# An adaLN block with cached attention and a gated FFN: Q's weight sums and splits at other steps, two kinds of work on another engine, background jobs over other steps, and four stores for the last weight rows

## The chip, the cores and the metric

The kernel runs on one core of a Trainium2 chip. The metric is the device time of one execution in microseconds (us), as the median of several executions. A core has a tensor engine for matmuls (PE in the profile; PEld is its loading of stationary operands), a vector engine (VectorE, DVE), a scalar engine (ScalarE, ACT), GpSimd (POOL) and SyncE (SP), which here issues nearly all DMA transfers. Each engine works through its own instructions in program order and waits on semaphores for the others. SBUF is the on-chip memory of 128 partitions, PSUM the matmuls' accumulator, and DRAM tiles serve as scratch. Transfers are carried out by 16 DMA engines.

## The reference

The input x is 2048 x 576, the attention has 32 query heads on 16 key heads of 128 columns with only the last 512 cached keys, and the FFN has 4608 hidden columns. All is float32.

```
W = min(4096, max(256, Sk // 4))                       # 512
q = (x @ wq).reshape(B, Sq, Hq, Dh), heads first
scores = einsum("bhqd,bhkd->bhqk", q, k[last W]) * Dh ** -0.5
o = einsum("bhqk,bhkd->bhqd", softmax(scores), v[last W]);   A = o @ wo
B(h) = (sigmoid(h @ w_gate) * (h @ w_up)) @ w_down

sa, ca, ga, sb, cb, gb = (silu(c) @ w_mod) in six rows of 576
h = layernorm(x) * (1 + ca) + sa
x = x + ga * A(h)
h = layernorm(x) * (1 + cb) + sb
x = x + gb * B(h)
```

## The kernel before

**Precision.** A float32 product is made of three matmuls in a faster type: each operand is split into a rounded high part (hi, a copy on ScalarE) and what is left (lo, a subtraction on GpSimd or VectorE), and `three` (line 283) multiplies hi by lo, lo by hi and hi by hi. So every matrix that goes to TensorE costs a copy and a subtraction somewhere.

**The step loop.** Attention works in 128 blocks (a head and a quarter of the rows, 512 of them); a block has four steps of 128 rows, so the loop (line 1297) runs over steps n from -8 to 512 and a few behind. In a step come, in program order: the functions that `at_n` hung on this step; Q matmuls (`u_some`); `scores(n + 2)` with the row maximum (neg) on VectorE; `transp(n)`, which transposes the probabilities and splits them into hi and lo (ptt); `expo(n + 2)`, the exponential (pp) on ScalarE, with the row sums; `pv` in two of four steps, probabilities times V into the tile ot, and after its second half VectorE's product of ot with rb, the broadcast of 1/sum, into ov; then the functions that `at_late` hung on the step. `keep_order` and `pin` tell the scheduler to keep an instruction in program order, so an engine's queue is in the main the order of this code, and all that follows an instruction that waits, waits too.

**1/sum.** At the end of a block VectorE takes the reciprocal (rs). `put_rs` stores it to DRAM (rscr, `at_late(n - 2)`, that is the end of the step in which it is made) and `get_rs` reads it back to all partitions (rb, two steps later). SyncE issues both, and rb waits for rscr to land.

**Q.** From the third block pair on, Q is made in units (30, one every 16 steps, `b_of` gives the first block) of seven products, after Strassen and Winograd, in place of eight. A unit u has a start step n = 4 b_of(u) - 10. `u_load` and `u_load_tail` fetch its columns of wq (tiles q and tr), `u_sum` makes the four weight sums S1 to S4 on GpSimd, `u_sum_tail` that of the last rows (tr), `u_tail_hi` and `u_tail_lo` split them (tw), `u_hi` and `u_lo` split the operands of product j into a tile sw of a ring of four. Line 864 and on hangs these on steps around n. `u_some` issues the products' matmuls by the table QUOTA, into the PSUM tiles qp and wo. When product j is done, `u_end` moves m1, u2, w aside or adds two of them into c; `u_out` copies c into Q's hi part (qt) and subtracts for the lo part, on VectorE for j = 4 and on GpSimd for 5 and 6.

**Background jobs.** The weights of the later phases are prepared in the shadow of attention, in three tiles of the size of x (rooms; tile x in the profile). A job "ab" (36 of them) loads a 128-column chunk of w_gate and w_up, makes four sums of it on GpSimd and stores seven planes (tile wsc in DRAM); a job "tail" (9) does so with the last 32 rows of each half for four chunks at once, with the hi and lo split done ahead; "wo" (16) and "down" (18), called wide, multiply by a modulation row, make sums, split, and store to wosc and dsc; "mod" (4) makes a modulation row: a load of w_mod, then ScalarE multiplies by silu(c) and GpSimd adds the products (`mod_sum`). `bg_load`, `bg_sums`, `bg_split` and `bg_store` are hung on steps after the job's start. A planner (line 1106 and on) gives each job a start step and a room: LIFE is the number of steps for which a room is held (and the step from which a wide job needs a second room), held_rooms what is taken otherwise, and `due` spaces the jobs.

**A tail job's stores** (line 1088). The four chunks lie side by side on 32 partitions each. Chunk q's rows go to four places in its tile of DRAM scratch, hi and lo in turn; lo needs two transfers (3 and 4 planes), so a part is six transfers, and the four parts stand in four steps, n + 9 to n + 12:

```
for to in range(4):
    for a, b, src in bg_pairs(k) if to % 2 else [(0, 7, hi)]:
        pin(nc.sync.dma_start(wsc[f + q][to * TQ : (to + 1) * TQ, a:b, 2, :], src[rows]))
```

**The end of the loop.** x is loaded again into the rooms; at N - 7 (N = 512) the pool wp is closed and a pool for the next phase opens, whose first operands `v_load`, `v_sum` and `v_split` prepare. For the last heads `sum_o` makes three sums on GpSimd. Behind the loop come the output projection (to 1950 us of the span) and the FFN, which the change leaves as they are.

The helper class at line 24 issues the instructions, so the profile puts nearly all of them down to L36; the tiles' names tell them apart.

Of the kernel before, what the change touches and what calls it, by code (L numbers as in the profile page):

```python
# [16 lines left out]
P = 128  # L17
# [27 lines left out]
def adaln_block_kernel(ctx: ExitStack, tc: tile.TileContext, x, k_cache, v_cache, wq, wo, w_gate, w_up, w_down,  # L45
# [100 lines left out]
    def mod_load(m, room):  # L146
        ws = []
        for j in range(2):
            w = bg_view(room, j * NC * D2, [NC, D2])
            cols = slice(m * D + j * D2, m * D + (j + 1) * D2)  # L150
            keep_order(nc.sync.dma_start(w, w_mod[: NC * P, cols].rearrange("(k p) n -> p k n", p=P)))
            ws.append(w)
        t = h_tile("wmt")[:TAIL]
        keep_order(nc.sync.dma_start(t, w_mod[NC * P :, m * D : (m + 1) * D]))
        return ws, t

    def mod_sum(loaded, k):
        ws, t = loaded
        for j in range(2):
            w = ws[j][:, k, :] if k < NC else t[:, j * D2 : (j + 1) * D2]  # L160
            kk = w.shape[0]
            keep_order(nc.scalar.activation(w, w, AF.Copy, scale=cexp[:kk, k : k + 1]))
            if k:
                nc.gpsimd.tensor_add(ws[j][:kk, 0, :], ws[j][:kk, 0, :], w)

    def mod_half(row, j, add, loaded):
        p = ps_pt()[:, :D2]
        pin(nc.tensor.matmul(p, ones, loaded[0][j][:, 0, :], start=True, stop=True))
        nc.vector.tensor_scalar(row[:, j * D2 : (j + 1) * D2], p, add, None, op0=OP.add)
# [503 lines left out]
    def expo(n):  # L673
# [5 lines left out]
        if i == TPB - 1:  # L679
            RS[b] = at.tile([P, TPB], F32, tag="rs", name="rs", bufs=3)  # L680
            nc.vector.reciprocal(RS[b], SUM[b])
            if b < NBLK - 2:
                at_late(n - 2, put_rs, b)
                at_late(n, get_rs, b)
# [3 lines left out]
            if last_of[half * H + hd] == b:  # L688
                if not summed(half, hd):
                    at_late(n + (2 if b == NBLK - 1 else 4), put_o, half, hd)  # L690
                elif hd % 2 == 0:
                    at_n(n + 4, sum_o, hd + 1)
                    at_n(n + 7, put_sx, hd + 1, (0, 1))
# [74 lines left out]
    def sum_o(hd):  # L768
# [4 lines left out]
        pin(nc.gpsimd.tensor_sub(s2, s1, e[:, :, 0]))  # L773
        pin(nc.gpsimd.tensor_sub(e[:, :, 1], e[:, :, 0], e[:, :, 1]))
# [136 lines left out]
    for b in range(2, NB):  # L911
        at_n(n1 - 60 + 4 * b, x_room, b)
        at_n(n1 + 40, x_room_end, b)
        for t in range(TPB):
            at_n(n1 - 59 + 4 * b + t, load_x, b, t)
# [92 lines left out]
    wsc = [dram.tile([P, 7, 3, P], F32, tag=f"wsc{f}", name=f"wsc{f}") for f in range(NF)]  # L1008
# [10 lines left out]
    def bg_load(k, rooms):  # L1019
        kind, f = k  # L1020
        if kind == "tail":
            raw = bg_view(rooms[0], 0, [4, P])
            BG[k] = raw, bg_view(rooms[0], 4 * P, [4, P]), bg_view(rooms[0], 8 * P, [7, P])
            for slot, w, r0 in ((0, w_gate, 2 * P), (1, w_gate, D2 + 2 * P), (3, w_up, 2 * P), (2, w_up, D2 + 2 * P)):
# [16 lines left out]
    def bg_sums(k, part):  # L1041
        kind, f = k
        if kind in ("ab", "tail"):
            if kind == "tail":
                r, m, hi = BG[k]
                x0, x1, x2, x3 = [r[:, i] for i in range(4)]
                s1, s2, s4, s3 = [m[:, i] for i in range(4)]
            else:
                x0, x1, x2, s1, s2, s4, s3, x3 = [BG[k][:, i] for i in range(8)]
# [19 lines left out]
        pin(nc.gpsimd.tensor_sub(t1, b12, b11))  # L1069
        pin(nc.gpsimd.tensor_sub(t2, b22, t1))  # L1070
        pin(nc.gpsimd.tensor_sub(t3, b22, b12))
        pin(nc.gpsimd.tensor_sub(t4, b21, t2))

    def bg_pairs(k):
        r, m, hi = BG[k]
        return [(0, 3, r[:, 0:3, :]), (3, 7, m)]

    def bg_split(k, part):
        if k[0] == "tail":
            r, m, hi = BG[k]  # L1080
            a, b, v = ((0, 3, r[:, 0:3]), (3, 7, m))[part]
        else:
            a, b = ((0, 4), (4, 8 if k == ("down", NF // 2 - 1) else 7))[part]
            v, hi = BG[k][0][:, a:b], BG[k][1]
        pin(nc.scalar.activation(hi[:, a:b].bitcast(F32R), v, AF.Copy))
        pin(nc.gpsimd.tensor_sub(v.bitcast(F32R), v, hi[:, a:b]))
# [19 lines left out]
    LIFE = {"ab": (9, None), "tail": (13, None), "wo": (11, 6), "down": (11, 6), "mod": (12, None)}  # L1106
    held_rooms = {0: [(-99, 29), (n1 - 53, n1 + 1)], 1: [(-99, 22), (n1 - 49, n1 - 6)],
                  2: [(-99, 25), (n1 - 26, n1)]}
    plan = []

    def room_for(a, b, but=None):
        fits = [(max([e for s, e in held_rooms[r] if e <= a], default=0), r) for r in held_rooms
                if r != but and all(e <= a or s >= b for s, e in held_rooms[r])]
        return max(fits)[1] if fits else None

    mods = [("gate1", 2, 0.0), ("scale", 4, 1.0), ("shift", 3, 0.0), ("gate", 5, 0.0)]
    mod_at, mod_due = {}, [30, 52, 80, 116]
    n, due = 22, 22.0
    while jobs or wide or mods:
# [743 lines left out]
```

## Time and profile before

| what | value |
| --- | --- |
| time, median of 3 runs | 3202.26 us (3201.67 to 3204.27) |
| the profiled execution's own time | 3205.68 us |
| its span in the profile | 3203.9 us |
| granted TensorE clock, mean | 0.986 |
| DMA over the span | 571.40 MB, 178 GB/s |
| HBM read / written | 394.33 MB / 173.70 MB |

The span is divided into the step loop (to about 1610 us), the output projection (to 1950 us) and the FFN. Busy time says how much of the span an engine executed something; the idle time in front of an instruction is put down to the one that released it last ("<-"). The granted clock is the share of full speed at which TensorE was allowed to run. DMA shares are of the core's 16 DMA engines.

### The profile page before, as it was taken

How to read it: one execution, taken by the hardware profiler on the slowest of the kernel's cores; microseconds unless marked ns; L12 is line 12 of the kernel's file. 1: busy time of each engine (PE TensorE's matmuls, PEld its weight loads, DVE VectorE, ACT ScalarE, POOL GpSimd, SP SyncE). 2: the span in 40 equal slices, each digit the busy share in tenths (PEclk: the TensorE clock that was granted, in tenths of full speed). 3: DMA queues.
4: the chain of work that ended last, by engine and by line, in shares of the span. 5: the costliest groups of instructions: out<-in, count | busy, mean ns of one | idle time of the engine just before them, and what ended most of it. 6: DMA issues, size and time to landing. Idle time of an engine off the chain costs nothing.

```text
span 3203.9 us, 50611 instructions
## 1 busy us (share of the span) xinstructions
PE 3052.6 (95%) x16981; PEld 2610.6 (81%) x16981; DVE 2190.0 (68%) x3845; ACT 1749.0 (55%) x3658; POOL 1914.0 (60%) x1836
## 2 busy tenths in 40 slices
PE   9988999899999898989999999999999999999999
PEld 7776777777777776767799998888888888888888
DVE  7666666687776665657678877666666686666667
ACT  5666566567666555555544465444444554444443
POOL 5566676634767767776255513676665566656565
PEclk9999999999999999999999999999999999999999
DMA  4575766662676766667754765655555565555554
GB/s 113 161 206 173 216 191 197 197 181 62 197 210 197 205 191 199 203 200 227 226 184 176 306 234 170 192 159 167 167 144 147 157 196 146 147 144 142 144 139 121
DMA packets 465636, 571.40 MB, mean 178 GB/s; under 512 B 51040, under 2 KB 414048, under 8 KB 456672
## 3 DMA queue, kind: packets, MB, share of 16 engines
q1 hardware_dynamic: 464240, 567.64, 59.5%
q8 instruction: 134, 2.20, 0.3%
q14 instruction: 126, 1.03, 0.1%
q10 hardware_dynamic: 1136, 0.53, 0.1%
HBM read 394.33 MB, written 173.70 MB: 177 GB/s over the span
## 4 chain that ended last, share of the span: by engine, by line
PE 49%; DVE 1%; POOL 1%; issue 0%; DMA 0%; ACT 0%; SPq 0%; DVEq 0%; POOLq 0%; ACTq 0%
PE a L36 20%; PE w L36 13%; PE c L36 10%; PE b L36 5%; PE ot L36 0%; DVE x L36 0%; PE st L36 0%; POOL x L36 0%; DVE v L36 0%; DMA rb<-rscr 0%; DVE sw L36 0%; POOL vs L36 0%; POOL hl L36 0%; DVE ov L36 0%; DVE ptt L36 0%
## 5 line engine op out<-in xcount | busy, mean ns | idle before, releaser
L36 DVE TENSOR_TENSOR x<-w,x 128x288 f32<-128x288 f32 x964 | 420.7, 451 | 249.2 <-PE w L36 248.1
L36 PE MATMUL a<-hc,sw 128*128 128x512 f32 x2016 | 583.5, 395 | 1.6 <-DVE v L36 1.5
L36 PE MATMUL st<-kt,qt 128*128 128x512 f32 x1536 | 477.6, 414 | 52.8 <-ACT pp L36 50.0
L36 DVE TENSOR_TENSOR ptt<-st,ptt 128x512 fp32r<-128x512 f32 x512 | 351.3, 686 | 213.0 <-ACT ptt L36 211.2
L36 ACT ACTIVATE ptt<-st 128x512 fp32r<-128x512 f32 x512 | 305.1, 596 | 340.0 <-PE st L36 338.0
L36 DVE TENSOR_REDUCE neg<-st 128x1 f32<-128x512 f32 x512 | 350.2, 684 | 151.9 <-PE st L36 149.8
L36 PE MATMUL ot<-ptt,vs 128*128 128x512 f32 (+1 forms) x2052 | 433.0, 352 | 13.7 <-DVE ptt L36 13.3
L36 ACT ACTIVATE pp<-st,neg 128x512 f32<-128x512 f32 x512 | 351.8, 687 | 79.5 <-DVE neg L36 77.9
L36 PEld LDWEIGHTS a<-hc,sw 128*128 128x128 f32 x2016 | 355.9, 188 | 42.3 <-DVE v L36 3.3
L36 PEld LDWEIGHTS st<-kt,qt 128*128 128x128 f32 x1536 | 283.9, 194 | 126.6 <-ACT pp L36 71.5
L36 POOL TENSOR_TENSOR sw<-sr,sw 128x256 fp32r<-128x256 f32 x245 | 198.9, 812 | 283.6 <-ACT sw L36 283.4
L36 PEld LDWEIGHTS ot<-ptt,vs 128*128 128x128 f32 x2052 | 317.1, 192 | 61.4 <-DVE ptt L36 26.2
L36 ACT ACTIVATE sw<-sr 128x384 fp32r<-128x384 f32 x504 | 257.8, 519 | 192.0 <-issue 89.8
L36 POOL TENSOR_TENSOR x<-x 128x288 f32<-128x288 f32 (+5 forms) x369 | 287.7, 795 | 69.2 <-DMA x<-in_B_w_up_dram 41.0
L36 PEld LDWEIGHTS st<-ident,pp 128*128 128x128 f32 x2048 | 260.8, 142 | 79.7 <-issue 4.8
L36 PE MATMUL st<-ident,pp 128*128 128x128 f32 x2048 | 317.4, 276 | 3.2 <-DVE rs L36 2.1
L36 PE MATMUL c<-hc,sw 128*128 128x512 f32 x1008 | 302.7, 393 | 0.0
L36 DVE TENSOR_TENSOR sw<-sr,sw 128x256 fp32r<-128x256 f32 x259 | 189.2, 731 | 142.6 <-ACT sw L36 117.9
L36 POOL TENSOR_TENSOR hl<-vs,hl 128x512 fp32r<-128x512 f32 x139 | 191.5, 1378 | 107.3 <-ACT hl L36 107.3
L36 POOL TENSOR_TENSOR x<-x,x 128x864 fp32r<-128x864 f32 (+3 forms) x111 | 207.4, 1874 | 68.6 <-ACT x L36 39.7
L36 PEld LDWEIGHTS c<-hc,sw 128*128 128x128 f32 x1008 | 181.5, 188 | 18.7
L36 PE MATMUL wo<-hTm,sw 128*128 128x512 f32 x540 | 164.2, 425 | 30.4 <-ACT m L36 15.5
(291 smaller groups left out, 6061.7 us busy)
## 6 DMA issues: line engine op xcount, KB each, us to landing
sr<-wsc SPq DMA_DIRECT2D x504, 192.0 KB
dsc<-x SPq DMA_DIRECT2D x34, 1008.0 KB
vr<-oscr SPq DMA_DIRECT2D x32, 1024.0 KB
rb<-rscr SPq DMA_DIRECT2D x126, 256.0 KB
oscr<-ov SPq DMA_DIRECT2D x63, 512.0 KB
wsc<-x SPq DMA_DIRECT2D x36, 896.0 KB
wosc<-x SPq DMA_DIRECT2D x32, 1008.0 KB
wh<-dsc SPq DMA_DIRECT2D x72, 288.0 KB
```

The lines of the kernel that those rows point to most:

```text
L36: i = got(*args, **kw)
```

## The change

It has these parts.

1. Q's units: loads, sums, tail sums and the splits of the operands stand on other steps. The tail's sum leaves the step of its copy, and the copies for products 0 to 6 go from steps (-4, -3, -1, 0, 3, 6, 8) to (-7, -6, -3, -2, 3, 5, 7) around the unit's start; a low part still comes one step behind.
2. The low part of Q is always made on VectorE (`u_out_lo`); it was on GpSimd for two of three.
3. A modulation row's sum is made by VectorE alone, 5 instructions a row on 576 columns, with one load in place of two, and on later steps.
4. `get_rs` is issued one step earlier.
5. Wide jobs: sums in three steps, splits at +7 and +8, store at +9; tail jobs: splits at +7 and +8, all stores at +9. LIFE and the planner follow: 12 steps for wide, 10 for ab, 11 for tail and mod, and the planner takes the first of a series of spacings with which all jobs end before step N - 30.
6. A tail job's 24 stores become 4, each of which writes one of the four places for all four chunks; the DRAM tiles of four chunks are one tile for that.
7. At the loop's end: x in pieces of a quarter block, the next phase's first load and sums three steps earlier, and `sum_o` over three steps.

```diff
     def mod_sum(loaded, k):
...
+        w, t = loaded
+        if k == 0:
+            pin(nc.vector.tensor_scalar(w[:, 0], w[:, 0], cexp[:, 0:1], None, op0=OP.mult))
+            return
+        v = w[:, k] if k < NC else t
+        a, n = w[: v.shape[0], 0], v.shape[0]
+        pin(nc.vector.scalar_tensor_tensor(a, v, cexp[:n, k : k + 1], a, op0=OP.mult, op1=OP.add))
...
-    def u_out(b, eng):
+    def u_out(b):
         t, c = q_tile(b), u_temp("c")
         keep_order(nc.scalar.activation(t[:, 0, :], c, AF.Copy))
+
+    def u_out_lo(b, c, eng):
+        t = QT[b]
         pin(eng.tensor_sub(t[:, 1, :], c, f32(t[:, 0, :])))
...
-            at_late(n + 3 if j == 6 else n, u_out, b + j - 3, nc.vector if j == 4 else nc.gpsimd)
+            eng = nc.vector
+            m = n + 3 if j == 6 else n
+            at_late(m, u_out, b + j - 3)
+            at_late(m, u_out_lo, b + j - 3, u_temp("c"), eng)
...
                 at_late(n - 2, put_rs, b)
-                at_late(n, get_rs, b)
+                at_late(n - 1, get_rs, b)
...
         for kk in range(2):
-            at_n(n - 11 + kk, u_load, u, kk)
-        at_n(n - 9, u_load_tail, u)
+            at_n(n - 12 + kk, u_load, u, kk)
+        at_n(n - 13, u_load_tail, u)
         for i in range(4):
-            at_n(n - 5 + i, u_sum, u, f"S{i + 1}")
-        at_n(n - 2, u_sum_tail, u)
+            at_n(n - 8 + i, u_sum, u, f"S{i + 1}")
+        at_n(n - 4, u_sum_tail, u)
         at_n(n - 2, u_tail_hi, u)
         at_n(n - 1, u_tail_lo, u)
-        for j, m in enumerate((-4, -3, -1, 0, 3, 6, 8)):
+        for j, m in enumerate((-7, -6, -3, -2, 3, 5, 7)):
...
-    wsc = [dram.tile([P, 7, 3, P], F32, tag=f"wsc{f}", name=f"wsc{f}") for f in range(NF)]
+    wsc4 = [dram.tile([4, P, 7, 3, P], F32, tag=f"wsc{f}", name=f"wsc{f}") for f in range(NF // 4)]
+    wsc = [wsc4[f // 4][f % 4] for f in range(NF)]
...
         if kind == "tail":
-            hi = BG[k][2]
-            q = part
-            rows = slice(q * TQ, (q + 1) * TQ)
-            for to in range(4):
-                for a, b, src in bg_pairs(k) if to % 2 else [(0, 7, hi)]:
-                    pin(nc.sync.dma_start(wsc[f + q][to * TQ : (to + 1) * TQ, a:b, 2, :], src[rows]))
+            src = BG[k][0 if part % 2 else 2][:, 0:7]
+            pin(nc.sync.dma_start(wsc4[f // 4][:, part * TQ : (part + 1) * TQ, :, 2, :], src))
...
-        for part in range(2):
+        for part in range(3 if two else 2):
             at_n(n + (4 if kind == "tail" else 3) + part, bg_sums, k, part)
-            if kind != "ab":
-                at_n(n + 6 + (1 if two else 2) * part, bg_split, k, part)
+        for part in range(0 if kind == "ab" else 2):
+            at_n(n + 7 + part, bg_split, k, part)
+            at_n(n + 7 + part, bg_split_lo, k, part)
         for part in range(4 if kind == "tail" else 1):
-            at_n(n + (6 if kind == "ab" else 8 if two else 9) + part, bg_store, k, part)
+            at_n(n + (6 if kind == "ab" else 9), bg_store, k, part)
...
-            at_n(n + 3 + c, lambda m, c: mod_sum(wm[m], c), m, c)
+            at_n(n + 5 + c // 2, lambda m, c: mod_sum(wm[m], c), m, c)
```

**What moves in SyncE's queue.** Around the stores of the first tail job (steps 47 to 50 before, 48 now) SyncE had the following rows; wsc_298 and on are chunks' tiles of DRAM scratch (one tile for four chunks after the change), x_101 is a room, rscr and rb are the 1/sum on its way to DRAM and back, oscr takes finished attention output.

```order
L36 DMA rscr_282<-rs 128x4 [waits DMAHW2_49,DVE_49]
L36 DMA wsc_298<-x_101 224x1x128 [waits DMAHW3_49,Activation_49]
L36 DMA wsc_298<-x_101 32x3x128 [waits DMAHW4_49,Pool_49]
L36 DMA wsc_298<-x_101 32x4x128 [waits DMAHW5_49,Pool_49]
L36 DMA wsc_298<-x_101 224x1x128 [waits DMAHW6_49]
L36 DMA wsc_298<-x_101 32x3x128 [waits DMAHW7_49]
L36 DMA wsc_298<-x_101 32x4x128 [waits DMAHW0_49]
L36 DMA oscr_0_283<-ov 512x1x256 [waits DMAHW1_49,DVE_49]
L36 DMA rb<-rscr_282 128x512 [waits DMAHW2_49]
```

Now, from the same rscr on:

```order
L36 DMA rscr_282<-rs 128x4 [waits DMAHW5_49,DVE_49]
L36 DMA rb<-rscr_282 128x512 [waits DMAHW6_49,DMAHW5_49]
L36 DMA oscr_0_283<-ov 512x1x256 [waits DMAHW7_49,DVE_49]
L36 DMA wsc_298<-x_101 4x224x128 [waits DMAHW0_49,Activation_49]
L36 DMA wsc_298<-x_101 4x224x128 [waits DMAHW1_49,Pool_49]
L36 DMA wsc_298<-x_101 4x224x128 [waits DMAHW2_49]
L36 DMA wsc_298<-x_101 4x224x128 [waits DMAHW3_49]
L36 DMA wsc_299<-x_102 896x1x256 [waits DMAHW4_49,Pool_49]
L36 DMA rscr_279<-rs 128x4 [waits DVE_49]
L36 DMA rb<-rscr_279 128x512 [waits DMAHW6_49,DMAHW5_49]
```

The first six of 24 small stores stood between rscr and rb (18 more follow them); now rb follows rscr at once, all four large stores come behind, and the next block's rscr and rb stand directly after them and a store of an ab job.

**What moves in GpSimd's queue.** Around the sums of the second unit GpSimd had the following; sS tiles are S1 to S4, q tiles raw weights, tr and tw the tail's sum and split, qt Q's low part, x_102 a room with a modulation row's sum.

```order
L36 TENSOR_TENSOR qt<-c,qt 128x512
L36 TENSOR_TENSOR sS_1545<-q_1294 128x256
L36 TENSOR_TENSOR sw<-q_1294,sw 128x256
L36 TENSOR_TENSOR x_102<-x_102 128x288 x2
L36 TENSOR_TENSOR sS_1545<-q_1325,sS_1478 128x256
L36 TENSOR_TENSOR tr<-tr 128x128
L36 TENSOR_TENSOR x_102<-x_102 128x288 x2
L36 TENSOR_TENSOR tw<-tr,tw 64x384
```

Now the same sums read:

```order
L36 TENSOR_TENSOR sS_1422<-q_1240 128x256
L36 TENSOR_TENSOR sw<-q_1240,sw 128x256
L36 TENSOR_TENSOR x_101<-x_101 128x256 x2
L36 TENSOR_TENSOR sS_1422<-q_1276,sS_1365 128x256
L36 TENSOR_TENSOR x_101<-x_101 128x256 x2
L36 TENSOR_TENSOR tr<-tr 128x128
L36 TENSOR_TENSOR sw<-sS_1365,sw 128x256
L36 TENSOR_TENSOR tw<-tr,tw 64x384
```

The low part of Q and the modulation adds are gone from this queue; in their places stand a room's sums (x_101) and the low part of a product's operand (sw).

More of the change, by code (lines that the diff above doesn't have):

```diff
@@ L692, in expo @@
                     at_n(n + 4, sum_o, hd + 1)
+                    for k in range(2):
+                        at_n(n + 5 + k, sum_o2, hd + 1, k)
                     at_n(n + 7, put_sx, hd + 1, (0, 1))
@@ L1043, in bg_sums @@
         if kind in ("ab", "tail"):
[L1044 to L1049, printed above, removed]
+            v = BG[k][0] if kind == "tail" else BG[k]
+            x0, x1, x2, s1, s2, s4, s3, x3 = [v[:, i] for i in range(8)]
             if part == 0:
@@ L1080, in bg_split @@
             r, m, hi = BG[k]
[L1081 removed]
+            a, b = ((0, 3), (3, 7))[part]
+            v = r[:, a:b]
         else:
@@ L1104, in bg_store @@
                 pin(nc.sync.dma_start(to, BG[k][1 - i][:, :n]))
-    LIFE = {"ab": (9, None), "tail": (13, None), "wo": (11, 6), "down": (11, 6), "mod": (12, None)}
-    held_rooms = {0: [(-99, 29), (n1 - 53, n1 + 1)], 1: [(-99, 22), (n1 - 49, n1 - 6)],
+    LIFE = {"ab": (10, None), "tail": (11, None), "wo": (12, 7), "down": (12, 7), "mod": (11, None)}
+    held_rooms = {0: [(-99, 29), (n1 - 48, n1 + 1)], 1: [(-99, 22), (n1 - 44, n1 - 6)],
                   2: [(-99, 25), (n1 - 26, n1)]}
-    plan = []
@@ L1153, in adaln_block_kernel @@
+    plan, held_rooms, mod_at = next(got for r in range(40) for got in [make_plan(
+        jobs, wide, {k: list(v) for k, v in held_rooms.items()}, 1 - r / 50)] if got)
     for n, k, rooms in plan:
@@ L1278, in v_split @@
         t = late["b"].tile([P, 2, 4, P], F32R, tag="vh", name="vh", bufs=3)
-        nc.scalar.activation(t[:, 0], src, AF.Copy)
-        nc.vector.tensor_sub(t[:, 1], src, f32(t[:, 0]))
+        i = nc.scalar.activation(t[:, 0], src, AF.Copy)
+        j = nc.vector.tensor_sub(t[:, 1], src, f32(t[:, 0]))
+        if hold:
+            pin(i)
+            pin(j)
         VHL[v, s] = t
```

160 lines of the change are left out of this document (81 added, 79 removed).

## The prediction

> **What bounds the kernel now.** The page comes first: the span, the busy shares, and TensorE's row of 40 slices.
>
> ```profile
> span 3203.9 us, 50611 instructions
> PE 3052.6 (95%) x16981; PEld 2610.6 (81%) x16981; DVE 2190.0 (68%) x3845; ACT 1749.0 (55%) x3658; POOL 1914.0 (60%) x1836
> PE   9988999899999898989999999999999999999999
> ```
>
> TensorE is busy for 95% of the span, so only about 150 us of idle time can be won on it, and the eights stand in the left half. The windows say how much lies where (columns: us, busy time of PE, PEld, DVE, ACT and POOL, granted clock, DMA share, GB/s).
>
> ```profile
> 90.00:1610.00 1520.00, 1384.08 (x7235) 1117.54 (x7234) 1018.49 (x1614) 927.55 (x2103) 952.90 (x975) 0.97 0.66 194
> 1610.00:3203.90 1593.90, 1585.86 (x9319) 1426.54 (x9317) 1106.86 (x2097) 768.81 (x1447) 911.53 (x816) 1.00 0.56 168
> ```
>
> The step loop, up to 1610 us, leaves TensorE idle for 1520 - 1384 = 136 us, and its clock there is 0.97, which is worth up to 0.03 x 1520 = 46 us more: 0.34 us of clock for each us of idle time. Behind 1610 us idle time is 8 us, and the diff touches nothing there but the first few tiles. So the change can win at most some 180 us, and all of it inside the loop. What TensorE waited for (us in all, times, longest) says which part of that the change can reach.
>
> ```profile
> PE st L36 <- ACT pp L36: 52.8, 28, 7.0
> PE wo L36 <- ACT m L36: 15.5, 15, 1.7
> PE ot L36 <- DVE ptt L36: 13.3, 14, 2.8
> PE qp L36 <- DVE c L36: 11.1, 10, 4.1
> PE qp L36 <- POOL sw L36: 9.9, 5, 5.6
> PE wo L36 <- POOL sw L36: 8.2, 8, 2.9
> ```
>
> These six are 110.8 us. ScalarE and VectorE are named, but they run in order, and the same view for 90 to 1610 us shows what they stand behind:
>
> ```profile
> ACT tw L36 <- POOL tr L36: 115.8, 28, 9.0
> DVE c L36 <- POOL qt L36: 22.8, 22, 5.0
> ACT x L36 <- DMA wsc<-x: 21.6, 3, 8.1
> DVE ov L36 <- DMA rb<-rscr: 29.9, 17, 4.2
> ```
>
> The hi copy of a unit's weight tail (tw) waits in 28 of 30 units for GpSimd's tail sum (tr), and every exponential (pp) queued behind it on ScalarE is late; the combination c waits for a low part of Q on GpSimd; a room's split waits for stores of the tail job before it; the attention output (ov) waits for the broadcast of 1/sum (rb). **GpSimd's and SyncE's lateness, passed on by ScalarE and VectorE, is what TensorE loses.**
>
> **The change, part by part.** *The unit's weight pieces* (steps of 1610 / 524 = 3.07 us): the tail sum runs at n-4 and its copy at n-2, not both at n-2, so GpSimd has 6.1 us. The mean wait is 115.8 / 28 = 4.1 us and the longest 9.0, so most of it goes. I count 75% of the 52.8 behind pp, the rest being room splits and loads of w_mod: 39.6. The low parts of sw for products 0 to 3 come 3 steps ahead in place of 0 or 1; 80% of 9.9 + 8.2 = 14.5. Moving product 3's copy out of step n, where m is copied as well, is worth 40% of 15.5 = 6.2. ptt's 13.3 comes partly by VectorE standing behind c and ov, and get_rs leaves a step earlier: 60%, 8.0.
>
> *Low part of Q on VectorE.*
>
> ```profile
> L36 POOL TENSOR_TENSOR qt<-c,qt 128x512 fp32r<-128x512 f32 x60 | 77.1, 1286 | 132.8 <-ACT qt L36 126.9 <-DMA raw<-in_A_k_cache_dram 3.0 <-PE wo L36 2.9
> L36 DVE TENSOR_TENSOR qt<-c,qt 128x512 fp32r<-128x512 f32 x30 | 30.3, 1008 | 1.4 <-ACT qt L36 1.4
> L36 DVE TENSOR_TENSOR c<-qp,m 128x512 f32<-128x512 f32 x30 | 20.7, 689 | 23.7 <-POOL qt L36 22.8 <-PE st L36 0.9
> ```
>
> GpSimd loses 60 x 1286 ns = 77 us and the 127 us in which its queue stood behind ScalarE's copy. VectorE gains 60 x 1008 ns = 60 us, and c no longer waits for GpSimd: 80% of 11.1 = 8.9. The new waits are VectorE's for the copy: 1.4 us in 30 in the second row, so 3 us for 60, with the neg and ptt of the next step queued behind. The trace also shows the price of two operands in SBUF: 1008 ns against 689 with one in PSUM. The Trainium skill, "SBUF — State Buffer", section "Who interferes with whom", puts this down to a read port that VectorE and GpSimd share, and says that such an instruction contends with GpSimd's reads. By it the 60 instructions would hold GpSimd up too, by at most the 319 ns that they are longer, 19 us in all beside the 77 that it loses, so the sum stays.
>
> *Modulation sums on VectorE.*
>
> ```profile
> L36 ACT ACTIVATE x<-x,cexp 128x288 f32<-128x288 f32 x32 | 15.6, 530 | 9.8 <-DMA x<-in_w_mod_dram 9.8
> L36 DVE TENSOR_TENSOR x<-x,x 128x288 f32<-128x288 f32 x24 | 16.7, 697 | 0.0
> ```
>
> ScalarE loses its 40 copies, 32 of them in the row, with the 9.8 us of waiting for w_mod; VectorE gets 20 instructions on 576 columns. No row has this form: twice the 288-column row, 1.4 us, is taken, so 28 us; the ends are 0.7 and 2.8 us each (14 and 56 us). It is spread over 12 steps in all. VectorE, 1018 us busy of 1520, becomes 1018 + 60 + 28 = 1106, 73%. I charge 10 us of TensorE for the load of 88 us; the ends are 0 (its slack hides it: 414 us stay idle) and 88 (each instruction ahead of a late neg).
>
> *Jobs over other steps.* Wide sums in three steps and splits at +7 and +8 free ScalarE from GpSimd. The 5 us of this are already in the 75%. The same number of bytes and operations remain, so I take 0, with ends of -10 and 10 us. The end of the loop (x in pieces, v_load three steps earlier) concerns the window around 1600 us; TensorE's total idle behind 1610 is 8 us, so 0 again, with ends -5 and 5.
>
> The gain of idle time is 39.6 + 14.5 + 6.2 + 8.0 + 8.9 = 77; with 5 us for a few shorter waits of the same kinds 82, less 10: 72. The clock adds 0.34 x 82 = 28. **Gain: about 100 us** (60 to 140).
>
> *The tail stores.* The page has the sizes, by queue and form (count, KB each):
>
> ```profile
> wsc<-x SPq DMA_DIRECT2D x72, 112.0 KB
> wsc<-x SPq DMA_DIRECT2D x72, 64.0 KB
> wsc<-x SPq DMA_DIRECT2D x72, 48.0 KB
> ```
>
> Nine tail jobs store 24 pieces each, 8 of each size: 1792 KB. The change writes the same bytes in 4 stores of 448 KB whose destination begins with a side of 4 chunks. How before's stores run, in one place where they stand close together:
>
> ```profile
> 1517.48 11.64 SPq L36 DMA_DIRECT2D wsc<-x  x12
> 1529.65 6.83 SPq L36 DMA_DIRECT2D wsc<-x  x12
> 1524.50:1525.50 1.00, 0.86 (x6) 0.49 (x5) 0.96 (x3) 1.00 (x4) 0.33 (x1) 1.00 1.12 324
> ```
>
> All 16 DMA engines are busy (1.12 of them by the records) and 324 GB/s flow: 1.835 MB take 5.7 us. SyncE needs 18.5 us to issue them, though, which the change shortens to four issues. The kernel has one other transfer whose DRAM side begins with 4 chunks, the four loads of a tail job:
>
> ```profile
> 614.90 1.21 SPq L36 DMA_DIRECT2D x<-in_B_w_gate_dram  x2
> 616.15 1.11 SPq L36 DMA_DIRECT2D x<-in_B_w_up_dram  x2
> 619.50:620.40 0.90, 0.43 (x3) 0.33 (x3) 0.90 (x2) 0.46 (x1) 0.90 (x2) 1.00 0.28 77
> DMA packets 155, 0.08 MB, mean 77 GB/s; under 512 B 5, under 2 KB 155, under 8 KB 155
> ```
>
> While nothing else moves (155 packets of 512 bytes, the loads' run), 0.28 x 16 = 4.5 engines are busy and 77 GB/s flow. **I take this rate for the new stores**: 1.835 MB / 77 GB/s = 23.8 us on a quarter of the engines. The ends are 5.7 us and 23.8.
>
> The Trainium skill, "DMA: Bandwidth & Descriptors", section "Why a DMA increments its semaphore by 16 and not by 1", says that the number of engines is the largest up to 16 that divides the slowest side of both access patterns, which for 4 and 128 is 4, and it makes no difference between loads and stores. The trace agrees for the loads (4.5 engines); no row here shows such a store. By it the stores take the 23.8 us; if only the SBUF side counted, 5.7.
>
> Every later transfer of SyncE that spreads over all engines has a share behind these stores, rscr and rb among them. What a late rb costs shows here:
>
> ```profile
> 573.05 0.57 SPq L36 DMA_DIRECT2D rb<-rscr  x1
> 579.71 1.05 DVE L36 TENSOR_TENSOR ov<-ot,rb 128x512 f32<-128x512 f32 x1 [4.13 <-DMA rb<-rscr]
> 581.42 0.73 PE L36 MATMUL qp<-hTm,sw 128*128 128x512 f32 x2 [4.06 <-DVE c L36]
> 581.00:584.40 3.40, 2.98 (x10) 2.43 (x11) 1.65 (x3) 2.00 (x5) 0.14 (x1) 0.72 0.79 226
> 584.40:587.80 3.40, 3.40 (x16) 2.44 (x15) 1.75 (x3) 1.36 (x4) 3.32 (x5) 0.78 0.53 176
> ```
>
> rb lands 6.7 us after its issue, ov waits 4.13 us for it, VectorE's queue stands, and TensorE waits 4.06: one for one. Then the clock is 0.72 and 0.78 for two windows: 0.50 x 3.4 = 1.7 us more. In a block of four steps, 1/sum is stored (rscr) at the end of the second step and, now, fetched (rb) at the end of the third; ov needs it 3 steps after that store, 9.2 us. The plan of the changed kernel puts the nine stores at steps 48, 110, 151, 198, 285, 339, 387, 435 and 482. Three of them (110, 198, 482) fall between rscr and rb: rb lands 23.8 + 0.8 us after the stores begin, and is wanted 9.2 us after: 15.4 late. Four (151, 339, 387, 435) fall behind an rb: the next rscr comes 9.2 us later, 14.6 us of backlog are left, rscr's landing costs SyncE 2.0 and rb 6.7, against 9.2: 14.1 late. SyncE's mean wait for it is 111.3 / 56 = 2.0:
>
> ```profile
> SPq L36 <- DMA rscr<-rs: 111.3, 56, 5.9
> ```
>
> The one at 48 leaves 17.7 of backlog (17.2 late), the one at 285 20.7 (20.2 late). In all 3 x 15.4 + 4 x 14.1 + 17.2 + 20.2 = 140 us, and 9 x 1.7 = 15 for the clock. **Loss: 155 us** (100 where part of the backlog is used up before a block wants anything, 200 where the next block's loads are late as well).
>
> **The sum.** The profiled execution took 3205.68 us, of which 3203.9 are the span; the median of the runs shown is 3202.26, 3.4 less. 3205.7 - 100 + 155 = 3261 against the profiled one, 3257 against the median; I give 3255. The forecast's own range is 3190 to 3330.
>
> **The rivals.** *All engines after all.* If a store spreads by its 128 partitions, the tail's stores take 5.7 us, four issues replace SyncE's 18.5 us, and the loss is gone: 3202 - 100 = 3100. For it: every store in this trace fills all engines. Against it: none of them has a side of 4, and the one kind of transfer that has it doesn't. The point from which it decides is a loss of 100 us, 11 a tail in place of 17; that is 6 us less of stores, 17.7 us, so a rate of some 104 GB/s.
>
> *Four engines, but the lateness is half hidden.* ov has two banks of PSUM (ot), and a stall of TensorE delays the next 1/sum too. With half the loss, 78 us, the time is 3202 - 100 + 78 = 3180. Against it stands the pair above, one for one.
>
> *The gain doesn't come.* GpSimd still has its sums in one queue; where tr stays behind room work, or VectorE's 88 us stand ahead of neg and ptt, two thirds of the gain go: 3202 - 33 + 155 = 3324. For it: VectorE at 73% in a loop where each step needs it three times. Against it: 77 us and all waits for ScalarE's Q copy leave GpSimd.
>
> **How the numbers follow.** Forecast 0.50 (3190 to 3330, around 3255); all engines 0.24 (3100); half hidden 0.10 (3180); no gain 0.16 (3324). A difference of 0.2%, 6.4 us, is about what can be told from none. Faster comes from the second, most of the third and little of the first: 0.30; the same 0.05; slower 0.65. The range goes from 3100 to 3340: below it lies half of the second case, above it a quarter of the last and a little of the first.
>
> **What would show it.** In the changed profile the wait of tw for tr is below 30 us in all, and c's for GpSimd's qt is gone; if not, the gain's largest terms are wrong. In the stretch behind each tail's stores the DMA share is near 0.25 to 0.3 with about 77 GB/s for some 20 us, and ov waits for rb by more than 10 us in nine places, 140 us in all with 4.2 as the longest before; if the share is near 1 there, the loss is wrong and the first rival holds. TensorE's wait for DVE c or ptt grows by as much as ov's for rb. VectorE's qt group has 90 instructions near 1.0 us; if it shows more than 1.3, the third rival gains.

## The result, and the profile after

The changed kernel takes 3256.61 us (median of 4 runs, 3253.84 to 3260.35) against 3201.97 for the kernel before: a ratio of 1.017 with a 95% interval of 1.0152 to 1.0187, so 1.7% slower. The forecast was 3255.

The page and the windows of the changed kernel, to be read against those of before (columns as there: us, busy time of PE, PEld, DVE, ACT, POOL, granted clock, DMA share, GB/s):

```profile
span 3254.4 us, 50348 instructions
PE 3034.7 (93%) x16981; PEld 2605.7 (80%) x16981; DVE 2251.7 (69%) x3925; ACT 1741.1 (53%) x3618; POOL 1832.6 (56%) x1744
PE   9979797979989797979899999999999999999999
90.00:1610.00 1520.00, 1321.74 (x6961) 1075.06 (x6961) 1043.75 (x1640) 893.09 (x2007) 857.75 (x873) 0.94 0.60 183
```

TensorE has as many matmuls as before. In the same 1520 us of the loop it gets through 6961 of them, where it was 7235; it is idle for 198 us where it was 136, and the clock is 0.94, not 0.97. In the row of slices seven sevens and two eights stand between the nines of the left half, where before had six eights. There are nine tail jobs. TensorE's waits over the span (us, times, longest) have another shape too:

```profile
PE st L36 <- ACT pp L36: 68.3, 29, 16.8
PE ot L36 <- DVE ptt L36: 60.1, 14, 17.2
PE st L36 <- DVE ptt L36: 35.9, 6, 17.8
PE qp L36 <- DVE c L36: 14.5, 15, 1.7
PE wo L36 <- DVE qt L36: 9.6, 8, 3.6
...
PE wo L36 <- POOL sw L36: 2.7, 1, 2.7
```

The number of waits has hardly grown, but the longest is 17.8 us where it was 7.0: a few long stalls. The waits for m (15.5) are gone from the list's head and those for sw have shrunk from 18.1 to 2.7 + 2.1. Three of the waits behind them, from 90 to 1610 us:

```profile
POOL x L36 <- DMA x<-in_B_w_up_dram: 138.1, 18, 24.0
DVE ov L36 <- DMA rb<-rscr: 123.1, 30, 17.9
ACT x L36 <- DMA wsc<-x: 31.9, 2, 18.7
```

ov's wait for the broadcast of 1/sum went from 29.9 us to 123.1, GpSimd's for loads of w_up from 41.0 to 138.1, and ScalarE's for stores out of a room (wsc) is now two long waits. ScalarE's wait of tw for tr (115.8 before) and VectorE's of c for GpSimd's qt (22.8) are in this view no more. One tail job shows how a stall comes about; SyncE's timeline from 1236 us on (start, us of issuing):

```profile
1236.77 0.32 SPq L36 DMA_DIRECT2D rscr<-rs  x1
1238.99 0.32 SPq L36 DMA_DIRECT2D rb<-rscr  x1
...
1239.87 17.84 SPq L36 DMA_DIRECT2D wsc<-x  x4
1257.82 6.37 SPq L36 DMA_DIRECT2D dsc<-x  x2
1266.48 1.76 SPq L36 DMA_DIRECT2D x<-in_B_w_gate_dram  x2
...
1270.38 0.56 SPq L36 DMA_DIRECT2D rscr<-rs  x1
...
1274.32 0.34 SPq L36 DMA_DIRECT2D rb<-rscr  x1
```

The same time in windows of 4 us, with the first of them before the stores' stretch has settled:

```profile
1240.00:1244.00 4.00, 3.92 (x22) 2.91 (x20) 3.50 (x6) 4.00 (x10) 4.00 (x5) 1.00 0.57 165
1244.00:1248.00 4.00, 3.98 (x19) 3.28 (x20) 2.45 (x4) 3.50 (x9) 4.00 (x4) 1.00 0.27 78
...
1260.00:1264.00 4.00, 4.00 (x23) 3.11 (x21) 1.39 (x3) 2.09 (x5) 0.00 (x0) 1.00 0.27 82
1264.00:1268.00 4.00, 0.15 (x1) 0.00 (x0) 0.00 (x0) 0.08 (x1) 0.00 (x0) 0.93 1.00 386
1268.00:1272.00 4.00, 0.00 (x0) 0.00 (x0) 0.00 (x0) 0.00 (x0) 0.00 (x0) 0.50 0.90 268
...
1280.00:1284.00 4.00, 2.04 (x7) 1.88 (x8) 4.00 (x7) 1.49 (x4) 2.67 (x2) 0.50 0.98 311
1284.00:1288.00 4.00, 4.00 (x12) 3.02 (x12) 1.02 (x3) 0.79 (x3) 3.73 (x6) 0.51 0.40 88
```

And VectorE and TensorE at its end:

```profile
1258.72 0.18 DVE L36 RECIPROCAL rs<-sum 128x4 f32<-128x4 f32 x1 [0.31 <-ACT pp L36]
1279.83 1.05 DVE L36 TENSOR_TENSOR ov<-ot,rb 128x512 f32<-128x512 f32 x1 [17.93 <-DMA rb<-rscr]
1281.96 1.09 PE L36 MATMUL st<-ident,pp 128*128 128x128 f32 x4 [17.81 <-DVE ptt L36]
```

From 1244 to 1264 us a quarter of the DMA engines is busy (0.27) and 78 to 82 GB/s flow: the four stores. SyncE issues the four in 17.84 us, and the two dsc stores behind them in 6.37. The reciprocal is there at 1258.72, but its rscr is issued at 1270.38, 11.7 us later, rb at 1274.32, and ov starts at 1279.83. TensorE stands for 17.81 us, and at 1284 its clock is still 0.51.

Not every tail stops TensorE in this way. Its longest gap behind each of the nine tails is 11.0, 16.8, 9.4, 15.5, 13.1, 15.5, 17.8, 17.2 and 13.9 us, 130 us in all, and the tail above is the longest. At the fourth to the eighth VectorE's ov waits for rb, 14.0 to 17.9 us each and 80 us in all; at the ninth it waits 13.9 us, which the profile puts down to a load of K issued right behind rb. At the first three ScalarE is the one that waits:

```profile
195.97 1.16 ACT L36 ACTIVATE x<-x 128x1152 fp32r<-128x1152 f32 x1 [13.14 <-DMA wsc<-x]
396.45 1.16 ACT L36 ACTIVATE x<-x 128x1152 fp32r<-128x1152 f32 x1 [18.73 <-DMA wsc<-x]
539.16 0.63 ACT L36 ACTIVATE vs<-raw 128x512 fp32r<-128x512 f32 x1 [12.67 <-DMA raw<-in_A_v_cache_dram]
```

In the first two the split of a wide job waits for stores out of a room, in the third a copy of V waits for a load that SyncE issues behind the tail's stores.

### The profile page after: what moved, and what is told of

Same layout as the page of the kernel before. It is cut to its first block, busy times and chain, and to the rows that moved or that the text cites. A ratio compares the mean times of both kernels' runs of the same rounds, so it can differ in the third digit from the quotient of the medians.

```text
span 3254.4 us, 50348 instructions
## 1 busy us (share of the span) xinstructions
PE 3034.7 (93%) x16981; PEld 2605.7 (80%) x16981; DVE 2251.7 (69%) x3925; ACT 1741.1 (53%) x3618; POOL 1832.6 (56%) x1744
## 4 chain that ended last, share of the span: by engine, by line
PE 50%; DVE 2%; issue 2%; DMA 1%; POOL 1%; SPq 1%; ACT 1%; DVEq 0%; ACTq 0%; POOLq 0%
PE a L36 20%; PE w L36 12%; PE c L36 10%; PE b L36 5%; PE st L36 1%; PE ot L36 1%; SPq L36 1%; POOL x L36 1%; DMA rb<-rscr 1%; DVE x L36 1%; PE wo L36 0%; DVE sw L36 0%; PE qp L36 0%; DVE vh L36 0%; DMA wb<-wosc 0%
## 5 line engine op out<-in xcount | busy, mean ns | idle before, releaser
L36 POOL TENSOR_TENSOR x<-x 128x288 f32<-128x288 f32 (+5 forms) x345 | 273.3, 810 | 156.1 <-DMA x<-in_B_w_up_dram 138.1
L36 POOL TENSOR_TENSOR x<-x,x 128x288 f32<-128x288 f32 (+3 forms) x111 | 206.9, 1870 | 91.3 <-ACT x L36 77.2
L36 DVE TENSOR_TENSOR ov<-ot,rb 128x512 f32<-128x512 f32 x128 | 136.4, 1065 | 145.5 <-DMA rb<-rscr 123.1
```

Source lines behind the costliest of these rows:

```text
L36: i = got(*args, **kw)
```

## Experiments

Twelve kernels were run. A ratio is to the kernel before on the same chip, with its 95% interval; kernels on different chips are compared by their ratios, and 0.001 is 3.2 us.

### The same bytes in other shapes

**by_chunk.** Each store of 448 KB is cut into one per chunk, in the same step and place.

```diff
-            pin(nc.sync.dma_start(wsc4[f // 4][:, part * TQ : (part + 1) * TQ, :, 2, :], src))
+            for q in range(4):
+                rows = slice(q * TQ, (q + 1) * TQ)
+                pin(nc.sync.dma_start(wsc[f + q][part * TQ : (part + 1) * TQ, :, 2, :], src[rows]))
```

> The changed kernel, with each of a tail's four stores of 448 KB cut into one per chunk: 16 stores of 112 KB, same bytes, same step, same place in SyncE's queue, and a destination that begins with 32 rows. Theory (a side of 4 puts the stores on 4 engines, and rb stands behind them): the nine long gaps of TensorE, 136 us, and the lower clock behind them, up to 45 us, go: 3080 to 3125 us. Rival (the place decides: all of a tail's bytes in one step ahead of the next rscr): 3230 us or more, since 16 issues take SyncE longer than 4. Rival (VectorE's added load or the other steps cost it): within 30 us of 3257.

Measured: 3140.59 us, ratio 0.9779 (0.9765 to 0.9794). The direction is the theory's; the time is 16 us above its range. The nine stalls are gone: ov's longest wait for rb is 4.2 us again. At one tail SyncE needs 13.7 us for the 16 issues; whether this is what keeps the time above the range was not tested. Row of SyncE's timeline:

```profile
1159.14 13.70 SPq L36 DMA_DIRECT2D wsc<-x  x16
```

**rows_first.** A tail's rows lie on the partitions in the order (row, chunk), and four chunks' scratch has the row outermost, so that four stores and four loads a tail remain, but each begins with a long side.

```diff
-    wsc4 = [dram.tile([4, P, 7, 3, P], F32, tag=f"wsc{f}", name=f"wsc{f}") for f in range(NF // 4)]
-    wsc = [wsc4[f // 4][f % 4] for f in range(NF)]
+    wsc4 = [dram.tile([P, 4, 7, 3, P], F32, tag=f"wsc{f}", name=f"wsc{f}") for f in range(NF // 4)]
+    wsc = [wsc4[f // 4][:, f % 4] for f in range(NF)]
...
-                src = w[r0 : r0 + TQ, f * P : (f + 4) * P].rearrange("r (q n) -> q r n", q=4)
+                src = w[r0 : r0 + TQ, f * P : (f + 4) * P].rearrange("r (q n) -> r q n", q=4)
...
-            pin(nc.sync.dma_start(wsc4[f // 4][:, part * TQ : (part + 1) * TQ, :, 2, :], src))
+            to = wsc4[f // 4][part * TQ : (part + 1) * TQ, :, :, 2, :].rearrange("r q c n -> (r q) c n")
+            pin(nc.sync.dma_start(to, src))
```

> The changed kernel, with a tail's rows in another order on the partitions (row, then chunk) and the scratch tile of four chunks laid out with the row ahead of the chunk: still four stores of 448 KB and four loads a tail, but both begin with a long side (896 and 32). Theory: as with 16 stores, 3080 to 3125 us, and a few us better, since the loads no longer run at 77 GB/s and SyncE issues 4 stores in place of 16. Rival (the size of a store or the place decides, not its outer side): as the changed kernel, within 20 us of 3257.

Measured: 3111.91 us, ratio 0.9686 (0.9671 to 0.9701), as the theory has it; it beats both kernels. Size, number, step and place of the stores are those of the changed kernel, so none of these makes the loss. SyncE's timeline at one tail, the window over it, and the loop's window:

```profile
1282.66 7.58 SPq L36 DMA_DIRECT2D wsc<-x  x4
1282.60:1290.20 7.60, 7.16 (x38) 5.67 (x37) 5.91 (x10) 4.55 (x12) 5.99 (x6) 1.00 1.02 341
90.00:1610.00 1520.00, 1443.44 (x7988) 1194.78 (x7988) 1160.31 (x1809) 961.31 (x2134) 930.13 (x919) 1.00 0.68 205
```

All engines are busy at 341 GB/s. In the loop TensorE is idle for 77 us, and the clock is 1.00.

**side_of_two.** Each store is cut into two, with a side of 2 chunks.

```diff
-            pin(nc.sync.dma_start(wsc4[f // 4][:, part * TQ : (part + 1) * TQ, :, 2, :], src))
+            for q in (0, 2):
+                pin(nc.sync.dma_start(wsc4[f // 4][q : q + 2, part * TQ : (part + 1) * TQ, :, 2, :],
+                                      src[q * TQ : (q + 2) * TQ]))
```

> The changed kernel, with each tail store cut into two of 224 KB whose destination begins with a side of 2 chunks. Theory: 2 engines, half the rate (38 GB/s), 47.6 us a tail in place of 23.8; each of the nine gaps grows by some 24 us: 3257 + 215 = 3470 us (3400 to 3500). Rival (size or place): smaller pieces in the same place, 3257 within 20 us or less.

Measured: 3430.76 us, ratio 1.0689 (1.0669 to 1.0709), in the theory's range. SyncE's timeline at one tail, and two of the windows behind its start:

```profile
1182.50 39.02 SPq L36 DMA_DIRECT2D wsc<-x  x8
...
1231.64 0.47 SPq L36 DMA_DIRECT2D rscr<-rs  x1
1204.00:1208.00 4.00, 4.00 (x25) 3.32 (x23) 3.07 (x5) 2.65 (x7) 0.00 (x0) 1.00 0.14 43
1216.00:1220.00 4.00, 0.00 (x0) 0.00 (x0) 0.00 (x0) 0.00 (x0) 0.00 (x0) 0.90 0.14 43
```

Half the side, half the engines: 0.14 x 16 = 2.2, 43 GB/s, and issuing takes twice as long. With 4, 0.27 x 16 = 4.3 and 80 GB/s. In these runs the destination's outer side goes with the number of engines that are busy, and the rate with that number.

**before_four_stores.** The kernel before with the changed kernel's four stores (and the sums' place that they need) at step 9 of a tail job, and nothing else.

```diff
-            for to in range(4):
-                for a, b, src in bg_pairs(k) if to % 2 else [(0, 7, hi)]:
-                    pin(nc.sync.dma_start(wsc[f + q][to * TQ : (to + 1) * TQ, a:b, 2, :], src[rows]))
+            src = BG[k][0 if part % 2 else 2][:, 0:7]
+            pin(nc.sync.dma_start(wsc4[f // 4][:, part * TQ : (part + 1) * TQ, :, 2, :], src))
...
-            at_n(n + (6 if kind == "ab" else 8 if two else 9) + part, bg_store, k, part)
+            at_n(n + (6 if kind == "ab" else 8 if two else 9), bg_store, k, part)
```

> The kernel before with the new four stores of a tail job at its step 9 (and the tail's sums in one array, as they need), and nothing else of the change. Theory: the loss of the stores alone, 155 us by the prediction, on top of 3202: 3357 us (3300 to 3400). Rival (the loss comes from other parts, the stores relieve SyncE): 3202 or up to 20 us faster.

Measured: 3323.63 us, ratio 1.0344 (1.0329 to 1.036). The stores alone make the kernel before 113 us slower by the medians (3210.35 there), 110 by the ratio; the time is in the theory's range and below its middle, which stood for 155 us.

**before_rows_first.** The same with the stores and loads of rows_first.

```diff
-            pin(nc.sync.dma_start(wsc4[f // 4][:, part * TQ : (part + 1) * TQ, :, 2, :], src))
+            to = wsc4[f // 4][part * TQ : (part + 1) * TQ, :, :, 2, :].rearrange("r q c n -> (r q) c n")
+            pin(nc.sync.dma_start(to, src))
```

> The kernel before with four stores a tail at step 9 that spread over all engines (rows in the order of rows_first, loads too), and nothing else of the change. Theory (the prediction's zero for the stores' own relief of SyncE): ratio 0.995 to 1.0. Rival (the 24 stores held SyncE up, and the tail loads ran on 4 engines: part of what the change wins comes from here): 0.985 to 0.994.

Measured: 3184.69 us, ratio 0.9945 (0.9928 to 0.9961): 18 us faster than before, between the two ranges. A gain of zero is excluded by the interval, so the direction is the rival's; stores and loads were spread together, so how they share the 18 us is open. Against before_four_stores the spread is worth 1.0344 - 0.9945 = 0.040, 128 us. ScalarE's wait for tr from 90 to 1610 us, and TensorE's for pp over the span:

```profile
ACT tw L36 <- POOL tr L36: 112.4, 28, 9.0
PE st L36 <- ACT pp L36: 39.4, 26, 5.2
```

The wait for tr is nearly whole (115.8 before), and TensorE's wait for pp has still fallen from 52.8 to 39.4. ScalarE's wait of 21.6 us for the old stores is gone.

### What the rest of the change wins

**rows_first_again** repeats the base beside the next three kernels.

> The kernel rows_first once more, as the base on the same chip as the other three: ratio to before 0.967 to 0.972.

Measured: 3095.94 us, ratio 0.967 (0.9653 to 0.9688).

**tail_sum_back** undoes one line of rows_first.

```diff
-        at_n(n - 4, u_sum_tail, u)
+        at_n(n - 2, u_sum_tail, u)
```

> The kernel rows_first (ratio to before 0.9686) with the tail's weight sum back in the step of its copy (n-2, not n-4), and nothing else. Theory: this wait of ScalarE for GpSimd is the largest single term of the gain; ScalarE's wait of tw for tr, 0.3 us in rows_first, comes back to 80 to 120 us and some 20 to 40 us of TensorE with it: ratio 0.975 to 0.982. Rival (with Q's low parts and the modulation adds gone from GpSimd its queue is short enough): ratio within 0.002 of 0.9686.

Measured: ratio 0.9711 (0.969 to 0.9731), some 10 us slower than the two bases, with an interval that overlaps that of one of them. The wait itself hardly returned. ScalarE's wait for tr from 90 to 1610 us, and TensorE's for pp:

```profile
ACT tw L36 <- POOL tr L36: 22.5, 13, 4.4
PE st L36 <- ACT pp L36: 19.1, 28, 2.8
```

22.5 us, not 80 to 120, and TensorE's wait for pp is 19.1 as against 20.3 in rows_first. The rival is nearer.

**q_steps_back** puts all of Q's unit steps in rows_first where they were before.

```diff
-            at_n(n - 12 + kk, u_load, u, kk)
-        at_n(n - 13, u_load_tail, u)
+            at_n(n - 11 + kk, u_load, u, kk)
+        at_n(n - 9, u_load_tail, u)
...
-            at_n(n - 8 + i, u_sum, u, f"S{i + 1}")
-        at_n(n - 4, u_sum_tail, u)
+            at_n(n - 5 + i, u_sum, u, f"S{i + 1}")
+        at_n(n - 2, u_sum_tail, u)
...
-        for j, m in enumerate((-7, -6, -3, -2, 3, 5, 7)):
+        for j, m in enumerate((-4, -3, -1, 0, 3, 6, 8)):
```

> The kernel rows_first with all of Q's unit steps (loads, tail sum, sums S1 to S4, splits of the operands) as before the change. Theory (the terms 39.6 + 14.5 + 6.2 us and a third more for the clock come from these steps): about 80 us slower than rows_first, ratio 0.985 to 0.996. Rival (the gain comes from the work taken off GpSimd and ScalarE): under 20 us slower, ratio 0.969 to 0.975.

Measured: ratio 0.9744 (0.9728 to 0.9761), 0.006 to 0.007 or about 21 us behind the bases. The theory (80 us) falls. The waits of tw are 55.7 us here and cost little:

```profile
ACT tw L36 <- POOL tr L36: 55.7, 20, 6.4
PE st L36 <- ACT pp L36: 19.3, 27, 2.8
```

**q_low_gpsimd** puts 60 of the 90 low parts of Q back on GpSimd in rows_first.

```diff
-            eng = nc.vector
+            eng = nc.vector if j == 4 else nc.gpsimd
```

> The kernel rows_first with Q's low part of products 5 and 6 on GpSimd again (60 instructions). Theory (moving it frees the wait of c, 8.9 us and clock, and costs 7 us of VectorE's load): within 10 us of rows_first, ratio 0.967 to 0.972. Rival (VectorE at 73% is what is short): faster than rows_first by 10 us or more, ratio 0.965 or less. Rival (GpSimd's queue is what is short): slower by 15 us or more, ratio 0.973 or more.

Measured: ratio 0.9755 (0.9735 to 0.9775), about 25 us behind the bases. It is in the second rival's range: by it GpSimd's queue is what is short, not VectorE's time, and two waits bear that out. c waits for GpSimd for 39.4 us (22.8 before), and TensorE's wait of ot for ptt goes from 14.9 to 30.2.

**both_back** makes the last two edits together.

> The kernel rows_first with both of the two undone at once: Q's unit steps as before, and Q's low part of products 5 and 6 on GpSimd. Alone they cost about 0.006 and 0.007. Theory (they stand in for each other: either of them takes GpSimd's lateness off ScalarE's and VectorE's queues): more than the sum of the two, ratio 0.988 or more. Rival (they add up): 0.980 to 0.985. Rival (they share one cause that only one can lose): 0.976 to 0.979.

Measured: ratio 0.9808 (0.9794 to 0.9823), 0.0138 behind the base on the same chip, or 46 us by the medians. The two add up (0.0066 + 0.0077 against the mean of the bases), and the ratio is at the lower end of that rival's range. ScalarE's wait for tr and TensorE's for pp, as above:

```profile
ACT tw L36 <- POOL tr L36: 102.6, 29, 7.6
PE st L36 <- ACT pp L36: 24.8, 24, 3.9
```

The wait for tr is nearly as long as before the change (115.8), and TensorE's wait for pp is 24.8, not 52.8.

**before_q_parts** gives the kernel before Q's new unit steps and the low part on VectorE, and nothing else.

```diff
-            at_late(n + 3 if j == 6 else n, u_out, b + j - 3, nc.vector if j == 4 else nc.gpsimd)
+            eng = nc.vector
+            m = n + 3 if j == 6 else n
+            at_late(m, u_out, b + j - 3)
+            at_late(m, u_out_lo, b + j - 3, u_temp("c"), eng)
...
-            at_n(n - 5 + i, u_sum, u, f"S{i + 1}")
-        at_n(n - 2, u_sum_tail, u)
+            at_n(n - 8 + i, u_sum, u, f"S{i + 1}")
+        at_n(n - 4, u_sum_tail, u)
...
-        for j, m in enumerate((-4, -3, -1, 0, 3, 6, 8)):
+        for j, m in enumerate((-7, -6, -3, -2, 3, 5, 7)):
```

> The kernel before with the Q part of the change alone: its unit steps and Q's low part always on VectorE; 24 stores, modulation sums, wide jobs and the planner stay. Theory (these carry the gain, 77 us of idle time and the clock): 70 to 100 us faster, ratio 0.969 to 0.978. Rival (the wide jobs, the modulation sums and the stores carry half of it): 30 to 60 us, 0.981 to 0.991.

Measured: 3155.66 us, ratio 0.9857 (0.9842 to 0.9872): 47 us. It is the rival's range. Its waits (TensorE's over the span, ScalarE's from 90 to 1610 us) show what is left:

```profile
ACT tw L36 <- POOL tr L36: 1.6, 2, 1.0
ACT x L36 <- DMA wsc<-x: 28.8, 4, 9.0
ACT x L36 <- DMA x<-in_w_mod_dram: 11.2, 6, 5.7
PE st L36 <- ACT pp L36: 43.4, 28, 6.5
```

ScalarE's 115.8 us of waiting for tr are gone, and TensorE's wait for pp has only gone from 52.8 to 43.4. ScalarE's queue still has the waits for the tail's old stores and for w_mod.

**rb_later** fetches rb one step later in rows_first, as the kernel before does.

```diff
-                at_late(n - 1, get_rs, b)
+                at_late(n, get_rs, b)
```

> The kernel rows_first with the broadcast of 1/sum fetched one step later again. Theory (the earlier fetch saves some of the 30 us that ov waits): 5 to 10 us slower, ratio 0.970 to 0.972. Rival (issued right behind rscr it makes SyncE wait for rscr's landing, 241.7 us in rows_first against 111.3 before, and all transfers behind it with that): as fast or some us faster, ratio 0.969 or less.

Measured: ratio 0.9713 (0.9698 to 0.9729), some 11 us behind the two bases, with an interval that reaches into that of one of them. SyncE waits for rscr for 95.6 us instead of 241.7, as the rival says, but it wins no time by it; the theory's direction is the likelier, and its size is not settled.

## Why the prediction was right, and where it wasn't

**The loss.** The prediction said that stores with a side of 4 run on a quarter of the engines at 77 GB/s, 23.8 us a tail, that rb comes late by it, and that TensorE stands one for one. The trace after shows 0.27 and 78 to 82 GB/s, 20 us from 1244 on; by_chunk and rows_first take the loss away with the same bytes in the same step, and side_of_two doubles the time of issuing. By the mean ratio of the two rows_first runs (0.968) the spread is worth (1.017 - 0.968) x 3202 = 157 us; the sum had 155. With 16 stores it is 125, and on the kernel before 128, so 125 to 157 depending on what takes their place (rows_first spreads the tail's loads too). Against before's own 24 stores the four cost 110 us (before_four_stores), which is less than the 155 that the sum had for just this. The rule of the Trainium skill, "DMA: Bandwidth & Descriptors", section "Why a DMA increments its semaphore by 16 and not by 1", which gives 4 engines for a side of 4 and 2 for a side of 2, agrees for these stores: 4.3 and 2.2 by the DMA shares.

The step that was wrong in part is the way from the stores to TensorE. The sum had a late rb at all nine tails, 140 us. TensorE's nine gaps are 130 us, close to that, but ov waits for rb by more than 10 us at five tails (80 us), not nine; at the ninth it waits as long for a transfer that the profile names otherwise, and at the first three ScalarE waits for the stores themselves or for a load of V behind them. So the sum of the gaps agrees partly by luck. The one-for-one step holds at the tail shown, 17.93 for ov and 17.81 for TensorE. Nor did the sum have why rb was late there: it let rscr and rb stand in the DMA engines' queues behind the stores, and the trace shows SyncE itself held, 17.84 us for four issues, the two dsc stores and the loads behind that, and rscr issued 11.7 us after its reciprocal.

**The clock behind a stall** was put at 1.7 us each. At the tail shown, the clock is 0.50 and 0.51 in the two windows from 1280 to 1288, in which TensorE is busy for 2.04 and 4.00 us, so about 3 us are lost, an estimate from these two rows. The term is small; its example was a stall of 4 us, for stalls of 9 to 18.

**The gain.** The sum had 100 us. rows_first is (1 - 0.968) x 3202 = 102 us faster than before, and its idle time in the loop is 77 us, 59 less than before, with the clock at 1.00 for 0.97. Of the 102 us, 18 come from the stores and loads being spread (before_rows_first), so what the sum counted is worth about 85 us there, in its range of 60 to 140. Its parts did not hold:

- *Q's steps and low parts* were most of it: 39.6 + 14.5 + 6.2 + 8.9 = 69 us of idle, and with a third for the clock some 90. Both ways of testing give half: 46 us (both_back) and 47 us (before_q_parts). The step that failed is "75% of the 52.8 behind pp" put down to tw's wait for tr. In before_q_parts that wait is gone and 43.4 of the 52.8 remain; in both_back it is 102.6 us long and TensorE waits 24.8 for pp; in before_rows_first it is 112.4 long and 13 us of TensorE's wait go all the same, with the old stores. So ScalarE's longest wait was in the main slack, and a wait upstream was counted as TensorE's.
- *Moving the low part to VectorE* was forecast as worth 8.9 us of waits less its load. It is worth about 25 (q_low_gpsimd). VectorE had room: 1160 us busy of 1520 in rows_first, with TensorE idle less than before. The new waits for ScalarE's copy, put at 3 us, are 31.6 in the changed kernel; q_low_gpsimd has 3.0 of them and is the slower. The price of 1008 ns for two operands in SBUF was read off a mean: in before 13 of the 30 subtractions take 0.68 to 0.70 us, as long as the other form, and the rest 0.75 to 2.22, so it isn't a fixed price of the form.
- *The stores' relief of SyncE* was put at 0 apart from the loss; together with the spread of the loads it is worth 18 us (before_rows_first).
- *Jobs, modulation sums, the loop's end and rb's step* were put near 0. 102 - 47 - 18 = 37 us are left for them and for what the parts win only together; only rb's step among them was tried alone. The waits for the tail's stores and for w_mod, which before_q_parts still has (28.8 and 11.2), are in their domain: in rows_first the first is 2.5. How the 37 us divide is open.

**The rivals.** *All engines after all* would have given 3100; it is what the stores do in rows_first, 3111.91 and 3095.94, so its price was right and its condition false. *Half hidden* falls in the changed kernel with the nine gaps, 130 us where the sum had 140 and half would be 70. *The gain doesn't come* falls with rows_first.

**The signs it named.** The wait of tw for tr and that of c for GpSimd's qt are gone, the DMA share at the tail shown is 0.27 for some 20 us, and VectorE's 90 subtractions take 932 ns on average: these came. The nine waits of ov for rb didn't, as said above.

**The errors that met.** The net of 53 us came within 2 us, and that is partly luck. In the gain, Q's terms were too large by some 44 us (90 for 46) and the zeros too small by some 55 (18 + 37). And how the net divides depends on the order in which the parts are put in. On top of spread stores, the rest of the change wins 85 us and the slow stores cost 157. Put into the kernel before, the stores cost 110 us, and the rest of the change then wins 1.0344 - 1.017 = 0.0174, 56 us. By that order the sum's 155 and 100 are both about 45 us too large, and the two errors cancel. What the runs show is the net and the cause of the loss; they don't show that 155 and 100 are its two parts.

## What to carry to other kernels

Fewer, larger transfers are not cheaper by themselves: look at the outermost side of the DRAM pattern, since in these runs 4 and 2 there went with about four and two busy engines, and a layout with a long outer side kept the four issues and lost the stall. A transfer that runs on few engines is paid for by whatever stands behind it in the issuing queue or waits for the memory that it reads, here a small broadcast, a load of V and the split of another job. And a large wait on an engine that isn't the bottleneck is a guess at a gain, not a gain: take it away alone before counting it.

## What the runs showed of the hardware

- SyncE's issuing took longer where fewer engines were busy: at the seven tails where SyncE issued them alone, four stores of 448 KB took 17.2 to 19.8 us in the changed kernel (4.3 engines by the DMA share) and 4.1 to 7.8 in rows_first (16), and eight of 224 KB took 39.0 at the tail shown of side_of_two (2.2). At the 80 GB/s measured the four stores last about 23 us, an estimate, so issuing went on for most of that time, and rscr behind it was issued 11.7 us after its reciprocal.
- During a stall of 17.8 us the granted clock was 0.93 in the first window of 4 us and 0.50 in the second, and it was 0.51 in the window from 1284 to 1288, 2 to 6 us after work had begun again at 1281.96.
- ScalarE's wait for GpSimd's tail sum was 115.8 us in before and 1.6 in before_q_parts, with 9 us of difference in TensorE's wait for pp (52.8 and 43.4).
